# A Mamba-2 scan followed by a GELU feed-forward layer: batch transposes in two PSUM tiles, the last second-product by column halves, and a new instruction order

## The chip, the cores and the metric

The kernel runs on one core of one Trainium2 chip. The metric is device microseconds of that core, from an execution of the whole program, inputs and outputs in HBM. Lower is better. TensorE multiplies, VectorE (DVE), ScalarE (ACT) and GpSimd (POOL) do the elementwise work, and SyncE (SP) issues the DMA transfers.

## The reference

The program computes two layers, one after the other. First, a state-space scan over x (4 batches, 8 heads, 768 positions, 32 features), with decay a and matrices B and C (16 states each). A sequence is cut into chunks, and for each chunk

```
M       = (C B^T) * L                      # L[i,j] = product of a from j+1 to i, for i >= j, otherwise 0
y       = M x  +  (C state) * decay to i   # inside the chunk, and from the chunks before
state   = decay of the chunk * state + sum_j decay(j to end) * B_j x_j
```

Then y is laid out as 3072 tokens of 256 features, and

```
h   = y @ w_in                 # 256 -> 2048
g   = gelu_tanh(h)
out = g @ w_out                # 2048 -> 256
```

All inputs and the output are fp32; the kernel multiplies in bf16 and adds up in fp32.

## The kernel before

*Tiles.* A chunk is 128 positions, so a batch has 6 chunks and there are 24. Chunks go in units: the first two alone, then by twos, 13 units in all (`UNITS`, L126). A batch's decay is a running product (`f_clip`, `f_R`, `f_RT`, `f_recip`, L277 to L291), which VectorE multiplies into C and B of the whole batch (`f_mul`, L316, C first).

*One batch's preparation* (`sequence`, L607; `sequence0`, L628, for the first). TensorE transposes the scaled C and B (`f_T`: T_b_1 for C and T_b_0 for B, six 128x128 transposes each). For the batches after the first, both transposes go to banks 0 and 2 of one PSUM tile `gb` of four banks, by way of the list `T6` (L232). Evictions copy them to SBUF: `f_E` of C gives `ch`, of B gives `bh`. `f_F` makes `ce` from `ch`: two masked copies, one for even and one for odd heads. `f_N` transposes `bh` back chunk by chunk into bank 1 of `gb`, and `f_bn` evicts that as `bn`. For the first batch, `f_F0` reads the transposed C from PSUM directly, in two column ranges, and the transposes of B go to the one-bank tile `yb`.

*One unit.* `f_G` multiplies bh with ce into `gb`: the Gram matrices of the 8 heads, half of each bank for each chunk. `f_M` on VectorE multiplies them with the causal mask. `f_D` multiplies bn with x: the chunk's addition to the state. `f_S` and `f_SP` on VectorE carry the state on and spread it. `f_Y` adds the product of the states and of the masks into `yb`, and `f_yev` evicts that as `xm`, the input of the second layer. From unit 4 on, Y of a unit and D and G of the next are one node (YDG). `f_castx` turns a unit's x to bf16.

*The second layer.* `f_s1` multiplies a 128-row block of w_in's columns with a unit's tokens: groups of 512 output columns in one PSUM bank (pool `hp`, two banks; a few in the one bank of pool `o_ps`). `f_gelu` evicts each group on ScalarE. `f_s2` multiplies a chunk's g with w_out: 16 matmuls of 256 columns in four groups, into `o_ps` (two of the last four chunks: into `yb`). `f_oev` evicts them and `f_store` sends the chunk's 128 KB to HBM. The weights arrive as fp32 in two halves of w_in (1 MB each) and four quarters of w_out (512 KB each), and are cast in 512-column pieces (`f_wi`, `f_wo`: two pieces for each quarter of a matrix).

*The order.* Nothing is ordered by hand. Each step above is a node with an engine, a duration, dependencies and the buffers that it takes (`takes`, by pools with counts). `run_order` (L32) is a planner: it goes through planned time and, on each engine, takes of the nodes that can start the one with the lowest priority. The table `TUNE` gives each node its priority, `ENG` picks the engine for casts and evictions that may run on several. The outcome is the order in which instructions are emitted; each engine then runs its own in that order, and waits where a dependency asks for it. SP issues the loads in the planned order, and the stores in between. `emit_after` moves the emission of a batch's C eviction past the transpose of B. Where the plan has TensorE idle before the first product, filler matmuls with zero weights are put in (`idle`, L764).

Of the kernel before, what the change touches and what calls it, by code (L numbers as in the profile page):

```python
# [8 lines left out]
FP32 = mybir.dt.float32  # L9
BF16 = mybir.dt.bfloat16  # L10
# [4 lines left out]
class Node:  # L15


    def __init__(self, eng, dur, fn, deps=(), prio=0.0, done=0.0):
        self.eng, self.dur, self.fn, self.prio, self.done = eng, dur, fn, prio, done
        self.deps = [d for d in deps if d is not None]  # L20
        self.allocs = []
        self.after = 0.0
        self.emit_after = None
        self.start = self.end = None
# [7 lines left out]
def run_order(nodes, pools, hop=0.08, same=0.04, idle=None, wait=()):  # L32

    hist = {p: [] for p in pools}
    free = {}
    todo = list(nodes)
    order = []

    def est(n):
        t = 0.0  # L40
        for d in n.deps:
            if d.end is None:
                return None
            t = max(t, d.end + n.after
                    + (d.done + hop if d.eng != n.eng else 0.0 if n.eng == "PE" else same))
        for i, (pool, _) in enumerate(n.allocs):
            h, j = hist[pool], sum(p == pool for p, _ in n.allocs[:i])
            if len(h) + j >= pools[pool]:
                for d in h[len(h) + j - pools[pool]]:
                    if d.end is None:  # L50
                        return None
                    t = max(t, d.end + (same if d.eng == n.eng else hop))
        return t

    while todo:
        best = None
        cand = {}
        for n in todo:
            e = est(n)
            if e is not None:  # L60
                cand.setdefault(n.eng, []).append((e, n))
        assert cand, [(n.eng, n.prio, n.fn) for n in todo[:5]]
        for eng, c in cand.items():
            t = max(free.get(eng, 0.0), min(e for e, _ in c))
            if best is None or t < best[0]:
                best = (t, eng)
        t, eng = best
        ready = [(n.prio, e, i, n) for i, (e, n) in enumerate(cand[eng]) if e <= t + 1e-9]
        ready.sort(key=lambda r: r[:3])
        n = ready[0][3]  # L70
        if eng in wait:
            soon = [(e, m) for e, m in cand[eng] if t < e < t + n.dur - 0.1 and m.prio < n.prio - 5]
            if soon:
                e1 = min(e for e, _ in soon)
                fit = [r[3] for r in ready if t + r[3].dur <= e1 + 0.1]
                if fit:
                    n = fit[0]
                else:
                    t, n = min(((e, m) for e, m in soon if e <= e1 + 0.1),
                               key=lambda r: r[1].prio)  # L80
        if idle is not None and eng == "PE":
            x = idle(free.get(eng, 0.0), t)
            if x is not None:
                order.append((free.get(eng, 0.0), x, None))
        n.start, n.end = t, t + n.dur
        free[eng] = n.end
        for pool, by in n.allocs:
            hist[pool].append(by)
        todo.remove(n)
        order.append((t, n.fn, n))  # L90
    for n in nodes:
        if n.emit_after is not None:
            at = {r[2]: i for i, r in enumerate(order) if r[2] is not None}
            i, j = at[n], at[n.emit_after]
            if i < j and not any(r[2] is not None and r[2].eng == n.eng for r in order[i + 1:j]):
                order.insert(j, order.pop(i))
    return [(t, fn) for t, fn, _ in order]
# [3 lines left out]
def kernel(  # L101
# [10 lines left out]
    nc = tc.nc  # L112

    batch, H, S, D = x.shape
    N = B.shape[-1]
    Q = 128
# [115 lines left out]
    T6 = [gb[:, 2 * i, 0:S // 2].bitcast(BF16) for i in range(2)]  # L232
# [130 lines left out]
    def f_N(b, c0=0, c1=CPB):  # L363
        if c0 == 0:
            U[b]["n"] = (gb[:, 1] if b else psh.tile([128, 512], FP32, name="hp"))[:, 0:S // 2] \
                .bitcast(BF16)
        for c in range(c0, c1):
            nc.tensor.transpose(out=U[b]["n"][:, c * 128:(c + 1) * 128],  # L368
                                in_=U[b]["bh"][:, c * Q:(c + 1) * Q], identity=ident)
# [152 lines left out]

    def f_oev(gc, eng):
        o_sb = opool.tile([128, d_model], FP32, name="o_sb")
        if eng == "ACT":
            nc.scalar.activation(o_sb, ops.pop(gc), AF.Copy)  # L526
        else:
            nc.vector.tensor_copy(out=o_sb, in_=ops.pop(gc))  # L528
        outs[gc] = o_sb
# [40 lines left out]
    for item in FIRST.split() + [f"{t}{b}" if t in "CB" else f"x{CPB * b + int(t)}"  # L570
                                 for b in range(1, batch) for t in "CB012345"]:
        t, i = item[0], int(item[1:])
        if t in "CB":
            bl[i, int(t == "C")] = load(1.75, load_bc, i, int(t == "C"))
        elif t == "x":
            xl[i] = load(0.92, load_x, i)
        elif t == "i":
            win_l[i] = load(3.0, load_wi, i)
            win_l[i].done = 1.3
        else:  # L580
            won_l[i] = load(1.45, load_wo, i)
    cast = {"POOL": 0.6, "ACT": 0.62, "DVE": 0.45}
    for q in range(4):
        wi_n[q] = [add(cast, 0, f_wi, q, k, deps=[win_l[q // 2]], prio=-9 + 0.1 * q) for k in range(2)]
        wo_n[q] = [add(cast, 0, f_wo, q, k, deps=[won_l[q]], prio=20 + q) for k in range(2)]
    for h in range(2):
        win_l[h].takes("wf", *wi_n[2 * h], *wi_n[2 * h + 1])
        won_l[2 * h].takes("wf", *wo_n[2 * h], *wo_n[2 * h + 1])


    cl = add("DVE", 0.35, f_clip, deps=[an], prio=-90)
    R_ = add("DVE", 0.7, f_R, deps=[cl], prio=-89)
    RT_ = add("DVE", 0.53, f_RT, deps=[R_], prio=-88)
    rc1 = add("DVE", 0.47, f_recip, 0, 1, deps=[RT_], prio=-62)
# [12 lines left out]
    def sequence(b, after):  # L607
# [5 lines left out]
        tn[0].deps.append(tn[1])  # L613
        ev = {"DVE": 0.95, "ACT": 0.82}
        e1 = add(ev, 0, f_E, b, 1, 0, 128, deps=[tn[1], after], prio=q + 0.3)
        e1.emit_after = tn[0]
        e0 = add(ev, 0, f_E, b, 0, 0, 128, deps=[tn[0], after], prio=q + 0.5)
        ff = add("DVE", 0.74, f_F, b, deps=[e1], prio=q + 0.4)
        nn = add("PE", 0.34, f_N, b, deps=[e0, e1], prio=q + 0.6)
        bb = add({"ACT": 0.82, "DVE": 0.55}, 0, f_bn, b, 0, CPB, deps=[nn], prio=-45)  # L620
        tn[1].takes("gram", e1, e0)
        tn[1].takes("gram", e1, e0)
        nn.takes("gram", bb)
        nn.takes("gram", bb)
# [195 lines left out]
```

## Time and profile before

| | |
|---|---|
| median of 8 runs | 122.48 us (122.35 to 123.48) |
| the profiled execution's own time | 123.48 us |
| its span, from first to last instruction | 121.2 us |
| around the span | 2.28 us |
| TensorE busy | 111.3 us, 92% |
| ScalarE / VectorE / GpSimd busy | 75.6 / 63.5 / 20.1 us |
| DMA, the loads and stores together | 13.96 MB |
| last load landed | 53.32 us |
| last store landed | 120.15 us |

How to read the profile: times are microseconds from the span's start. "L502" is line 502 of the kernel. A group's name is the tile written, an arrow, and the tiles read. A row of the stretches gives its bounds, its length, then the busy time and number of instructions of PE (matmuls), PEld (weight loads), DVE, ACT and POOL, then TensorE's granted clock (1.00 is full), the mean busy share of the 16 DMA engines, and GB/s. A wait "A <- B" is idle time of A's engine that B ended. The chain is followed backwards from the last instruction, at each step to what released it. A matmul's row includes the time in which it drains, about 0.2 us; steps from one to the next are shorter than the duration.

### The profile page before, as it was taken

The page shows a single profiled execution, that of the slowest core. Times are in us where ns is not written, and L with a number is a line of the kernel's source. Part 1 is how long each engine was busy: PE and PEld are TensorE (multiplying, and loading weights), DVE is VectorE, ACT ScalarE, POOL GpSimd, SP SyncE. Part 2 cuts the span into 40 slices and gives each one's busy share as a digit, 9 for nine tenths or more (in the row PEclk, how much of TensorE's full clock was granted, in tenths as well). Part 3 has the DMA queues.
Part 4 walks back from the last instruction along what each step waited for, and adds up shares of the span by engine and source line. Part 5 has one row for each costly group of instructions (what it writes and reads, how often), then busy time and mean ns, then how long its engine had stood idle before and what let it go on. Part 6 is the DMA issues. An engine that isn't in the chain of part 4 may idle for free.

```text
span 121.2 us, 3506 instructions
## 1 busy us (share of the span) xinstructions
PE 111.3 (92%) x1507; PEld 98.2 (81%) x1507; DVE 63.5 (52%) x120; ACT 75.6 (62%) x143; POOL 20.1 (17%) x41
## 2 busy tenths in 40 slices
PE   4994959879899999999999999999999999999990
PEld 4993748758779898998889888897978999999970
DVE  5899677618579858907776719384745000000100
ACT  4138367554657686776866877766677778766410
POOL 7505078530240540222000000000000000000000
PEclk9999999999999999999999999999999999999999
DMA  1998999989999899851101101101110111011121
GB/s 46 277 319 174 300 270 300 267 186 227 217 214 165 137 213 239 136 108 50 43 2 49 43 1 49 43 0 49 43 49 0 43 43 40 12 43 43 43 87 43
DMA packets 38063, 13.96 MB, mean 115 GB/s; under 512 B 33824, under 2 KB 37024, under 8 KB 38048
## 3 DMA queue, kind: packets, MB, share of 16 engines
q1 hardware_dynamic: 37952, 13.69, 46.6%
q8 instruction: 11, 0.18, 0.6%
q10 hardware_dynamic: 96, 0.06, 0.2%
q14 instruction: 4, 0.03, 0.1%
HBM read 10.60 MB, written 3.15 MB: 113 GB/s over the span
## 4 chain that ended last, share of the span: by engine, by line
PE 75%; DMA 14%; SPq 3%; DVE 3%; ACT 2%; issue 1%; POOL 1%; DVEq 0%; POOLq 0%
PE hp L502 30%; PE o_ps L519 29%; DMA x_t<-in_x_dram 7%; DMA wf<-in_moe_w_in_dram 6%; PE yb L519 3%; PE gb L401 3%; PE yb L444 2%; PE yb L453 2%; PE gb L333 2%; DVE ch L266 2%; PE o_ps L783 1%; PE gb L368 1%; SPq L258 1%; SPq L159 1%; PE hp L422 1%
## 5 line engine op out<-in xcount | busy, mean ns | idle before, releaser
L510 ACT ACTIVATE gT<-hp 128x512 bf16<-128x512 f32 x94 | 52.7, 596 | 20.1 <-PE hp L502 19.8
L502 PE MATMUL hp<-xm,w_in_sb 128*128 128x256 bf16 (+1 forms) x400 | 51.3, 267 | 1.3 <-POOL w_in_sb L264 1.2
L519 PE MATMUL o_ps<-w_out_sb,gT 128*128 128x256 bf16 x352 | 47.6, 273 | 0.7 <-POOL w_out_sb L264 0.7
L502 PEld LDWEIGHTS <-w_in_sb 128*128 128x128 bf16 x416 | 41.9, 114 | 4.2 <-issue 1.6
L519 PEld LDWEIGHTS <-gT 128*128 128x128 bf16 x384 | 37.0, 98 | 5.4 <-issue 1.6
L411 DVE TENSOR_TENSOR m<-gb,tri 128x1024 bf16<-128x1024 f32 (+1 forms) x25 | 29.3, 1175 | 0.2
L528 DVE COPY o_sb<-o_ps 128x256 f32<-128x256 f32 x3 | 1.3, 425 | 26.3 <-PE o_ps L519 26.3
L264 POOL CAST x<-x_t 128x512 bf16<-128x512 f32 (+1 forms) x13 | 8.8, 682 | 23.8 <-DMA x_t<-in_x_dram 15.2
L471 DVE SCALAR_TENSOR_TENSOR s_new<-s_new,pend,hp 128x64 f32<-128x64 f32 x16 | 4.5, 279 | 12.6 <-PE hp L422 12.4
L783 PEld LDWEIGHTS <-wz 128*128 128x128 bf16 x105 | 7.7, 113 | 3.5 <-issue 1.8
L526 ACT ACTIVATE o_sb<-o_ps 128x256 f32<-128x256 f32 x19 | 7.3, 384 | 5.1 <-PE o_ps L519 2.8
L478 DVE SCALAR_TENSOR_TENSOR sp_new<-s_new,pend,bmask 128x256 bf16<-128x256 f32 x20 | 9.8, 490 | 0.1
L262 ACT ACTIVATE xm<-yb 128x512 bf16<-128x512 f32 (+1 forms) x13 | 7.3, 564 | 3.0 <-PE hp L422 2.6
L453 PE MATMUL yb<-m,x 128*32 128x128 bf16 x192 | 6.2, 220 | 0.0
L444 PE MATMUL yb<-ce,sp_new 128*32 128x128 bf16 x160 | 5.3, 221 | 0.0
L266 DVE COPY ch<-gb 128x768 bf16<-128x768 bf16 x3 | 2.9, 958 | 4.5 <-PE gb L333 4.5
L783 PE MATMUL yb<-wz 128*128 128x128 bf16 x35 | 3.7, 286 | 1.6 <-DVE warm L169 1.6
L264 POOL CAST w_out_sb<-wf 128x512 bf16<-128x512 f32 x7 | 4.5, 679 | 1.8 <-DMA wf<-in_moe_w_out_dram 1.8
L401 PE MATMUL gb<-ce,bh 32*128 32x256 bf16 x96 | 4.8, 273 | 0.0
L264 POOL CAST w_in_sb<-wf 128x512 bf16<-128x512 f32 x5 | 3.1, 664 | 9.2 <-DMA wf<-in_moe_w_in_dram 9.2
L469 DVE COPY s_new<-hp 128x64 f32<-128x64 f32 x4 | 0.9, 226 | 6.9 <-PE hp L422 6.9
L453 PEld LDWEIGHTS <-x 128*32 128x32 bf16 x192 | 3.7, 96 | 0.7 <-issue 0.6
(70 smaller groups left out, 64.7 us busy)
## 6 DMA issues: line engine op xcount, KB each, us to landing
x_t<-in_x_dram SPq DMA_DIRECT2D x24, 128.0 KB, 4.3
out_dram<-o_sb SPq DMA_DIRECT2D x24, 128.0 KB, 1.7
wf<-in_moe_w_in_dram SPq DMA_DIRECT2D x2, 1024.0 KB, 8.8
wf<-in_moe_w_out_dram SPq DMA_DIRECT2D x4, 512.0 KB, 6.6
bc_t<-in_C_dram SPq DMA_DIRECT2D x4, 384.0 KB, 4.5
bc_t<-in_B_dram SPq DMA_DIRECT2D x4, 384.0 KB, 5.2
a_t<-in_a_dram SPq DMA_DIRECT2D x1, 32.0 KB, 1.8
a_t<-in_a_dram ACTq DMA_DIRECT2D x1, 32.0 KB, 2.0
```

The lines of the kernel that those rows point to most:

```text
L262: nc.scalar.activation(o, i, AF.Copy)
L264: nc.gpsimd.tensor_copy(out=o, in_=i)
L401: nc.tensor.matmul(out=gb[:, g, 256 * k:256 * k + 256], lhsT=bh_of(gc)[32 * g:32 * g + 32], rhs=ce_of(gc)[32 * g:32 * g + 32], start=True, ...
L411: nc.vector.tensor_tensor(out=MT[gc][:, g0:g1], in0=gb[:, g0:g1, 256 * (k + half(u)):256 * (k + half(u)) + 256] .rearrange("p g (e t) -> p ...
L444: nc.tensor.matmul(out=y4[32 * j:32 * j + 32, k, w], lhsT=sp[:, 32 * h:32 * h + 32], rhs=ce_of(gc)[:, h % 2], start=first(j), stop=False, ...
L453: nc.tensor.matmul(out=y4[32 * j:32 * j + 32, k, w], lhsT=X16[u][:, k, 32 * h:32 * h + 32], rhs=m[:, h // 2, h % 2, :], start=first(j), st ...
L478: nc.vector.scalar_tensor_tensor(out=sp_new.rearrange("p (g d) -> p g d", g=4), in0=state[("s", gc)].rearrange("p (o d) -> p o d", o=1).to ...
L502: nc.tensor.matmul(out=hp[:, j * nt:(j + 1) * nt], lhsT=w_in_sb[:, kc].rearrange("p (q m k) -> p q k m", m=128, k=4)[:, fi // 4, fi % 4], ...
L510: nc.scalar.activation(gts[u][:, i * per:(i + 1) * per, 0:nt], hps.pop((u, i)).rearrange("p (j t) -> p j t", j=per), AF.Gelu_apprx_tanh)
L519: nc.tensor.matmul(out=ops[gc], lhsT=gts[u][:, fi, tt * Q:(tt + 1) * Q], rhs=w_out_sb[:, fi, :], start=(fi == 0), stop=(fi == NF - 1), ski ...
L526: nc.scalar.activation(o_sb, ops.pop(gc), AF.Copy)
L783: nc.tensor.matmul(out=bank[:, 384:384 + w], lhsT=wz[:, 0:128], rhs=r, start=True, stop=True)
```

## The change

- *PSUM tiles of the batch transposes.* For the batches after the first, the transposed B goes to `yb` and no longer to `gb`; N goes to `yb` as well. Only the transposed C stays in `gb`, and only the evictions of `ch` (one engine for each batch) and the masks read `gb`. The nodes take the matching pools. `emit_after` is gone.
- *The last chunk's second product* is made by halves of its columns: 16 matmuls of 128 columns into `o_ps`, then 16 into an `hp` bank, each half with its own eviction and its own 64 KB store.
- *Planned durations of the loads*: w_in's halves 2.6 and 3.4 instead of 3.0, their completion 1.25 instead of 1.3, that of w_out's quarters 1.2.
- *New priorities and engines* (`TUNE` and `ENG` are replaced as a whole), so that all engines' orders change up to about the sixth unit; from YDG_6 to the last chunk TensorE's order is the one of before.

The orders as they come out, where they matter most (SP's first loads; casts of weights, with the engine):

```
loads before:  C0 B0 w_in/0 x1 x0 w_in/1 x3 x2 w_out/0..3 x4 x5 C1 B1 x6 x7 B2 x8 x9 C2 ...
loads after:   C0 B0 x0 w_in/0 x1 w_in/1 x2 x3 x5 x4 w_out/0..3 C1 B1 x9 x6 x7 x16 x14 x8 x13 x10 x11 x12 x15 C2 B2 ...
POOL before:   wi_0_0 wi_1_0 x(0,1) wi_3_1 wi_2_1 wi_2_0 x(2) wo (7 pieces) x(3) ...
POOL after:    x(0) wi_0_0 wi_0_1 x(1) wi_1_1 wi_3_0 wi_2_1 x(2) x(3) wo (6 pieces) x(4) ...
w casts on ACT before: wi_0_1, wi_1_1 (ahead of and behind an eviction of ce)      after: wi_2_0 (behind gelu_0_1)
w casts on DVE before: wi_3_0, wo_3_1                                              after: wi_1_0, wi_3_1, wo_2_0, wo_3_0
TensorE before: ... D_2 G_3 s1_0_3 s1_1_2 Y_2 s2_0_0_0 s1_1_3 ... s1_2_4 s2_1_0_0 D_3 ... s1_2_7 Y_3 T_1_1 T_1_0 ... N_1 ... D_4 G_4
TensorE after:  ... s1_0_3 D_2 s1_1_2 G_3 Y_2 D_3 s1_1_3 s1_2_0 s1_2_1 s2_0_0_0 ... Y_3 s1_2_5 ... T_1_1 ... T_1_0 ... G_4 N_1 ... D_4
```

(s1_u_i is group i of the first product of unit u; s2_u_t_q quarter q of the second product of the unit's chunk t; wi_q_k and wo_q_k a piece of a weight's quarter q.) On VectorE, `mul_2_1` now stands behind the masks of unit 5 and ahead of S_6; the eviction of batch 1's C moved from VectorE to ScalarE.

The diff, without the two tables:

```diff
-    T6 = [gb[:, 2 * i, 0:S // 2].bitcast(BF16) for i in range(2)]
+    T6 = [yb[:, 0:S // 2].bitcast(BF16), gb[:, 2, 0:S // 2].bitcast(BF16)]
...
-            U[b]["n"] = (gb[:, 1] if b else psh.tile([128, 512], FP32, name="hp"))[:, 0:S // 2] \
+            U[b]["n"] = (yb if b else psh.tile([128, 512], FP32, name="hp"))[:, 0:S // 2] \
...
+    def f_s2_half(h, q):
+
+        u, w = NU - 1, d_model // 2
+        if q == 0:
+            ops["half", h] = (pso.tile([128, 512], FP32, name="o_ps") if h == 0 else
+                              psh.tile([128, 512], FP32, name="hp"))[:, 0:w]
+        for fi in range(4 * q, 4 * q + 4):
+            nc.tensor.matmul(out=ops["half", h], lhsT=gts[u][:, fi, Q:2 * Q],
+                             rhs=w_out_sb[:, fi, w * h:w * h + w], start=(fi == 0),
+                             stop=(fi == NF - 1), skip_group_check=True)
+
+    def f_oev_half(h, eng):
+        if h == 0:
+            outs["half"] = opool.tile([128, d_model], FP32, name="o_sb")
+        w = d_model // 2
+        copy(eng, outs["half"][:, w * h:w * h + w], ops.pop(("half", h)))
+
+    def f_store_half(h):
+        w = d_model // 2
+        nc.sync.dma_start(out=out[n_tokens - Q:, w * h:w * h + w],
+                          in_=outs["half"][:, w * h:w * h + w])
...
-            win_l[i] = load(3.0, load_wi, i)
-            win_l[i].done = 1.3
+            win_l[i] = load(2.6 + 0.8 * i, load_wi, i)
+            win_l[i].done = 1.25
         else:
             won_l[i] = load(1.45, load_wo, i)
+            won_l[i].done = 1.2
...
         e1 = add(ev, 0, f_E, b, 1, 0, 128, deps=[tn[1], after], prio=q + 0.3)
-        e1.emit_after = tn[0]
         e0 = add(ev, 0, f_E, b, 0, 0, 128, deps=[tn[0], after], prio=q + 0.5)
         ff = add("DVE", 0.74, f_F, b, deps=[e1], prio=q + 0.4)
-        nn = add("PE", 0.34, f_N, b, deps=[e0, e1], prio=q + 0.6)
+        nn = add("PE", 0.34, f_N, b, deps=[e0], prio=q + 0.6)
         bb = add({"ACT": 0.82, "DVE": 0.55}, 0, f_bn, b, 0, CPB, deps=[nn], prio=-45)
-        tn[1].takes("gram", e1, e0)
-        tn[1].takes("gram", e1, e0)
-        nn.takes("gram", bb)
-        nn.takes("gram", bb)
+        tn[1].takes("gram", e1)
+        tn[1].takes("gram", e1)
+        tn[0].takes("yb", e0)
+        nn.takes("yb", bb)
...
+            if gc == NCH - 1:
+                for h in range(2):
+                    for q in range(4):
+                        nd = add("PE", 0.226, f_s2_half, h, q, deps=[geln[u, 4 * n - 1], prev],
+                                 prio=PB + 45 + 10 * cs[0] + tt)
+                        if q == 0:
+                            first_n = nd
+                        prev = nd
+                    on = add({"DVE": 0.26, "ACT": 0.3}, 0, f_oev_half, h, deps=[prev], prio=-40)
+                    first_n.takes(("o", "hp")[h], on)
+                    sn = add("SP", 0.1, f_store_half, h, deps=[on], prio=gc)
+                    if h == 0:
+                        on.takes("ob", sn)
+                continue
```

## The prediction

> **What bounds the kernel now.** I read the page's shares first, then the busy times by stretch, then the chain that ended last, then who waited for whom, and last the tail.
>
> ```profile
> span 121.2 us, 3506 instructions
> PE 111.3 (92%) x1507; PEld 98.2 (81%) x1507; DVE 63.5 (52%) x120; ACT 75.6 (62%) x143; POOL 20.1 (17%) x41
> ```
>
> TensorE is busy 92% of the span; every other compute engine has a third or more to spare. The stretches (length, then busy time of PE, PEld, DVE, ACT, POOL, then clock, DMA share, GB/s) say where the missing 8% is:
>
> ```profile
> 15.90:17.90 2.00, 0.80 (x12) 0.54 (x10) 1.47 (x3) 1.37 (x3) 2.00 (x4) 1.00 0.96 296
> 17.90:26.55 8.65, 7.96 (x120) 6.60 (x120) 4.73 (x8) 5.17 (x10) 5.04 (x8) 1.00 0.92 258
> 26.55:35.85 9.30, 8.07 (x121) 6.70 (x120) 5.96 (x11) 5.39 (x10) 2.30 (x3) 1.00 1.01 219
> 35.85:54.59 18.74, 18.74 (x247) 16.84 (x246) 13.32 (x20) 13.30 (x25) 4.48 (x7) 1.00 0.93 166
> 54.59:117.92 63.33, 63.14 (x819) 56.58 (x818) 25.06 (x39) 43.35 (x83) 0.62 (x1) 1.00 0.11 37
> ```
>
> From 35.85 us to 117.92 us TensorE idles 0.2 us in all, at full clock: only less matmul work could shorten that. Between 15.90 and 35.85 it idles 1.20 + 0.69 + 1.23 = 3.1 us, while the DMA share is near 1. So the bound is loading first and TensorE afterwards, and an order can win what TensorE waits for before 36 us, plus the tail. Who ends those waits (total, times, longest):
>
> ```profile
> PE o_ps L783 <- ACT ce L350: 1.6, 1, 1.6
> PE hp L502 <- POOL w_in_sb L264: 1.2, 1, 1.2
> PE o_ps L519 <- POOL w_out_sb L264: 0.7, 3, 0.3
> PE hp L422 <- POOL x L264: 0.7, 1, 0.7
> PE gb L368 <- ACT bh L262: 0.6, 1, 0.6
> ```
>
> The chain (start, length, what) gives each its place:
>
> ```profile
> 10.43 0.63 ACT w_in_sb L262
> 11.06 0.58 ACT ce L350
> 11.69 1.11 PE o_ps L783 x17
> ...
> 17.71 8.86 DMA x_t<-in_x_dram
> ...
> 26.69 0.63 POOL x L264
> ...
> 31.67 0.97 DVE ch L266
> 32.66 0.82 ACT bh L262
> ```
>
> ScalarE took a weight cast that waited for w_in's first half (landed 10.41) ahead of the `ce` eviction; 17 filler matmuls waited behind that eviction. x of chunks 4 and 5 stood behind all of w_out and landed at 26.57, so D_3 waited. Batch 1's two evictions ran one after the other (`ch`, then `bh`), so N_1 waited.
>
> **The change, part by part.** I follow the new order on each engine, giving each instruction its row's duration, and compare the starts of the same TensorE blocks. Rows used: a 512-column group of first or second product 0.437; a two-chunk Y 0.45 to 0.56; T or N of six transposes 0.34; GELU 0.60; gram mask 1.22; S 0.28; SP 0.48; POOL cast 0.62; DVE cast 0.42; ACT cast 0.63; consumer about 0.2 after the last issue of its matmuls.
>
> *Landings.* Packets of one x load sum to 0.88 us of 16 engines, a B or C to 1.56, a w_out quarter to 1.58, a w_in half to 3.15. x0 now stands ahead of w_in's first half: 10.41 becomes at most 11.3, I take 11.2; x0 lands near 7.7. What precedes the second half is unchanged: 15.81. x4 and x5 move ahead of w_out and land near 18.7 instead of 26.6; the four quarters come 2 x 0.88 = 1.76 later, 20.5, 21.7, 24.1, 25.6. C1 and B1 follow the same bytes as before: 27.9 and 29.3.
>
> *Start.* The `ce` eviction no longer stands behind a weight cast, and no bn copy stands between the two halves of M_0 on VectorE: Y_0 moves from 13.03 to about 10.9. That is not the gain, for POOL now casts both parts of the first w_in quarter: 11.25 + 2 x 0.62 = 12.5, first product 12.55 instead of 13.89. Its third quarter waits for the landing at 15.81 as before. POOL has two casts of that half instead of three: 15.85 + 1.22 = 17.07, against 17.85. The ACT cast of it adds a wait: behind it on ScalarE stand the GELUs of chunk 1, ready near 15.2, now run 16.45 to 17.65; s1_0_2 needs the buffer freed at 17.05, no later than its weights, so this costs nothing, but it would if the landing slipped. s1_0_2 starts at 17.12. Then s1_0_3, D_2 (18.15), s1_1_2 (waits for a GELU, 18.3), G_3, Y_2 at 19.25 (before: 19.99, with the same work done): **-0.74**.
>
> *Middle.* D_3 comes at once, 19.8. s1_1_3 19.9, s1_2_0 20.65 (its xm eviction), s1_2_1 21.25, first second-product 21.8 (its w_out casts 20.5 + 1.24). Then no gap: Y_3 24.05 (masks end 23.5), s1_2_6 ends 25.45, s2_0_0_2 25.9. s2_0_0_3 needs casts of the last quarter, 25.65 + 0.62: 26.35, a wait of 0.45; ends 26.8. s1_2_7, s1_3_0, s2_1_0_0 end at 28.15. T_1_1 needs `mul_1_1` (0.90 from C1's 27.9): 28.85, a wait of 0.7. From there without a gap: s1_3_1, two groups, T_1_0 (30.55), three groups, G_4 32.25, N_1 ends 32.95; its `bh` eviction starts at 31.1 right after T_1_0, as `ch` now reads another PSUM tile and is done. By 35.85 the kernel before had the same done, and two groups and a D more (2 x 0.437 + 0.17 = 1.04). The new order is at that state at 32.95 + 1.04 = 33.99: **-1.86**, which holds the -0.74. The rest is the D_3 and N_1 waits, paid for with 0.45 and 0.7.
>
> *Until YDG_6* (54.59 before) both orders hold the same work, gapless before. Slack in the new one: the yb bank now serves T, N and Y in turn. YDG_5 at 43.0, T_2_0 at 48.8 (its mul ready 48.1), `bh` out at 50.45, N_2 50.9, its eviction by 52.4, YDG_6 52.75: the tightest slack is 0.4. *After YDG_6* the orders agree to the tail, except that batch 3's `ch` eviction need no longer wait for T_3_0; it removes the 0.17 wait at N_3: **-0.17**. Total matmul work is otherwise equal, filler excepted, which stands before the first product.
>
> *Tail.*
>
> ```profile
> 116.00 1.91 PE L519 MATMUL o_ps<-w_out_sb,gT 128*128 128x256 bf16 x16
> 118.00 0.42 DVE L528 COPY o_sb<-o_ps 128x256 f32<-128x256 f32 x1 [3.07 <-PE o_ps L519]
> ```
>
> 16 matmuls of 256 columns step at 109 ns: 1.75. Their place is taken by 32 of 128 columns, each with its own weight load. The nearest row is the transposes (fresh 128x128 weights, 128 columns): 12 in 0.67, 56 ns; first products of one chunk take up to 0.57 for 8, 71 ns. 32 x 60 = 1.92, +0.17 (+0.04 to +0.5). The Trainium skill, TensorE: Matmul & The Clock Gate, section Back-to-back issue gap, speaks against this part: a sustained stream of weight load and matmul pairs at N=128 is given as about 81 ns each, so 2.59 and +0.84. I take the trace. The first half's copy and store lie under the second's matmuls. The last copy shrinks: 128x256 took 425 ns, 128x64 226 (S from PSUM); a line through both gives 292: -0.13. The store took 1.37 from the end of its issue to landing; halving its bytes can spare only the data part. The skill's DMA: Bandwidth & Descriptors, in its table of the two cost components, gives a fixed part near 2.0 us, by which half the bytes spare 0.15; a whole store here took 1.7 with its issue, so that part is smaller here. I take -0.1 (0 to -0.3). Sum **-0.06** (+0.8 to -0.4).
>
> Sum: -1.86 - 0.17 - 0.06 = -2.09, some -2.0 as landings are known to a tenth at best. The profiled execution took 123.48 with a span of 121.2 (2.28 outside); the median is 1.00 below it. I put the change on the median: 122.48 - 2.0 = **120.5 us**.
>
> **Rivals.** *More:* C1 and w_out land early and the two waits (1.15) vanish: 119.4. For it: engine time of the bytes allows C1 1 us earlier; against it: landings have trailed it.
> *Half the gain:* x4 and x5 cost the w_out loads what they cost when they landed (23.82 to 26.57 = 2.75, not 1.76): every quarter another 1.0 later, TensorE waits for w_out at s2_0_0_3: 121.5. The scattered w_out row above speaks for it; against it, x2 and x3 added only 1.1.
> *No change:* waits move and do not vanish, since the same bytes must land and two hidden buffers alternate: GELUs held behind the ScalarE cast, and T_1 behind C1, return the 2.0: about 122.4. For it: until 29.3 us DMA runs near full in both. Against: by then TensorE waits for no later bytes.
> *Slower:* one mechanism. C2 and B2 are moved behind eleven x loads; `mul_2_1` stands ahead of S_6 and the next masks on in-order VectorE. C2 should land at 29.3 + 11 x 0.88 + 0.8 (two stores) + 1.56 = 41.4; VectorE reaches the mul at 41.8 and can wait to 42.8, with 0.4 more slack at N_2. From 43.2 each us late costs one; past 45.8 the kernel is slower by over 0.5%. At 46.2: 123.5. Against it: 4.4 us of lateness, more than any landing here strays.
>
> **How the numbers follow.** Forecast 0.55, more 0.06, half 0.12, no change 0.14, slower 0.13 (with all that makes VectorE or yb late in the like way). About 0.5% (0.61 us) is what a measurement of this kernel can tell from no change. Faster 0.55 + 0.06 + 0.12 = 0.73, same 0.14, slower 0.13. The forecast's own range, from its unknown costs (tail +0.8, slack, landings 0.5), is 119.7 to 121.5. The 8-in-10 range takes in more and half, and the near side of no change: 119.4 to 122.4.
>
> **What would show it.** Right: x waits on POOL near 26 us gone, no wait of D_3; second product's start near 21.8; N_1 and N_3 without a wait; TensorE idle between 15.9 and 33 us still about 2 us, on w_in, w_out and `mul_1_1`; YDG_6 near 52.8; the last 32 matmuls in about 1.9. Wrong: a wait of VectorE for C2 past 42.8; a wait of Y for yb; w_out waits over 1 us; 128-column matmuls stepping near 81 ns; w_in's second half landing after 16.5.

## The result and the profile after

The changed kernel took 121.27 us (median of 11, 120.38 to 122.21), beside 122.68 us for the kernel before in the same session (32 runs): ratio 0.9896, 95% interval 0.9865 to 0.9927, so 1.0% faster. The forecast was 120.5. Two more groups of runs gave 121.13 beside 122.41 (0.9897, 0.9825 to 0.9969) and 120.66 beside 122.57 (0.9834, 0.9784 to 0.9884). The ratios leave out executions that took over 1.5% more than the fastest of their kernel (1 of 12, 1 of 6 and 1 of 6 of the changed kernel); the medians hold them. The profiled execution took 121.33 us with a span of 119.5.

The page of the changed kernel: span, busy times, and the granted clock in 40 slices of 3 us.

```profile
span 119.5 us, 3521 instructions
...
PE 111.7 (93%) x1512; PEld 98.9 (83%) x1512; DVE 64.8 (54%) x121; ACT 76.6 (64%) x144; POOL 19.2 (16%) x40
...
PEclk9999959999999999999999999999999999999999
```

One slice has digit 5. The clock's record puts it at half speed for 3.41 us, from 14.47 to 17.89. No profile of the kernel before has such a window between start and last matmul.

Stretches of the changed kernel, columns as in the prediction (bounds, length, busy PE, PEld, DVE, ACT, POOL, clock, DMA share, GB/s):

```profile
10.00:14.00 4.00, 2.26 (x33) 1.46 (x30) 3.25 (x6) 1.35 (x4) 2.09 (x4) 1.00 1.06 337
14.00:18.00 4.00, 3.92 (x55) 2.96 (x56) 2.37 (x5) 1.71 (x3) 2.17 (x4) 0.57 0.90 152
18.00:22.00 4.00, 3.69 (x93) 3.07 (x90) 3.64 (x8) 3.22 (x6) 1.68 (x3) 1.00 0.99 334
22.00:36.00 14.00, 13.76 (x171) 12.14 (x170) 9.94 (x16) 11.04 (x20) 4.22 (x7) 1.00 0.97 210
36.00:55.00 19.00, 19.00 (x289) 16.79 (x288) 13.48 (x23) 13.60 (x26) 4.41 (x7) 1.00 0.87 185
55.00:114.00 59.00, 59.00 (x748) 53.48 (x745) 24.17 (x37) 41.42 (x79) 0.32 (x1) 1.00 0.10 33
```

After 36 us TensorE has no gap at all, where the kernel before still lost 0.2, and from 22 to 36 it loses 0.24. Between 14 and 18 us it is busy for 3.92 of 4.00 at a clock of 0.57: a group of the first product inside the window starts 0.81 before the next (17.01 to 17.82), where the same group took 0.44 at full clock in a second profile of this kernel.

TensorE's waits (total, times, longest):

```profile
PE o_ps L812 <- DVE w_in_sb L259: 0.9, 1, 0.9
PE o_ps L812 <- POOL w_in_sb L257: 0.8, 1, 0.8
PE yb L326 <- DVE bc L314: 0.3, 1, 0.3
PE hp L495 <- DVE s_new L464: 0.2, 1, 0.2
```

The waits for `x` (0.7), for w_out's casts (0.7) and for `bh` (0.6) are gone. Two waits stand ahead of filler matmuls (L812), which the new order places among the casts of w_in's first half; the last four stand behind the second POOL cast, ahead of the first product.

The chain of the changed kernel around the start (start, length, what):

```profile
3.48 8.37 DMA wf<-in_moe_w_in_dram
...
11.91 1.63 POOL w_in_sb L257 x2
13.54 0.04 issue
13.58 0.40 PE o_ps L812 x4
13.98 0.05 issue
14.02 0.69 PE o_ps L495 x8
...
15.90 0.61 ACT gT L503
...
18.06 0.61 ACT gT L503
...
18.70 0.61 PE hp L495 x8
```

The two POOL casts took 1.63, not 1.24, and the third quarter's product began at 18.70, behind a GELU that waited for products at half clock.

The tail of the changed kernel, in order of time (start, length, engine, line, tiles, shapes):

```profile
114.22 1.06 PE L523 MATMUL o_ps<-w_out_sb,gT 128*128 128x128 bf16 x16
...
115.11 1.06 PE L523 MATMUL hp<-w_out_sb,gT 128*128 128x128 bf16 x16
115.37 0.29 DVE L259 COPY o_sb<-o_ps 128x128 f32<-128x128 f32 x1 [2.22 <-PE o_ps L523]
...
116.20 0.29 DVE L259 COPY o_sb<-hp 128x128 f32<-128x128 f32 x1 [0.55 <-PE hp L523]
```

Sixteen matmuls of 128 columns start 0.89 apart from the next sixteen: 55.6 ns each.

### The profile page after: what moved, and what is told of

The parts are those of the page before. It is cut to its first block, busy times and chain, and to the rows that moved or that the text cites. A ratio compares the mean times of both kernels' runs of the same rounds, so it can differ in the third digit from the quotient of the medians.

```text
span 119.5 us, 3521 instructions
## 1 busy us (share of the span) xinstructions
PE 111.7 (93%) x1512; PEld 98.9 (83%) x1512; DVE 64.8 (54%) x121; ACT 76.6 (64%) x144; POOL 19.2 (16%) x40
## 4 chain that ended last, share of the span: by engine, by line
PE 82%; DMA 7%; DVE 2%; SPq 2%; POOL 1%; ACT 1%; issue 1%
PE hp L495 35%; PE o_ps L512 31%; DMA wf<-in_moe_w_in_dram 7%; PE yb L512 3%; PE gb L394 2%; PE yb L437 2%; PE yb L446 2%; POOL w_in_sb L257 1%; DVE sp_new L471 1%; ACT gT L503 1%; PE o_ps L495 1%; PE yb L361 1%; PE gb L326 1%; PE yb L326 1%; SPq L152 1%; PE hp L415 1%
## 5 line engine op out<-in xcount | busy, mean ns | idle before, releaser
L503 ACT ACTIVATE gT<-hp 128x512 bf16<-128x512 f32 x94 | 52.6, 595 | 16.2 <-PE hp L495 15.9
L495 PE MATMUL hp<-xm,w_in_sb 128*128 128x256 bf16 (+1 forms) x400 | 52.4, 270 | 0.6 <-DVE s_new L464 0.2
L512 PE MATMUL o_ps<-w_out_sb,gT 128*128 128x256 bf16 x336 | 45.2, 273 | 0.0
L512 PEld LDWEIGHTS <-gT 128*128 128x128 bf16 x368 | 35.8, 98 | 3.8 <-issue 0.2
L543 DVE COPY o_sb<-o_ps 128x256 f32<-128x256 f32 x2 | 0.8, 425 | 23.5 <-PE o_ps L512 23.5
L257 POOL CAST x<-x_t 128x512 bf16<-128x512 f32 (+1 forms) x13 | 8.1, 625 | 26.8 <-DMA x_t<-in_x_dram 19.5
L812 PEld LDWEIGHTS <-wz 128*128 128x128 bf16 x94 | 7.0, 112 | 3.8 <-issue 1.9
L255 ACT ACTIVATE xm<-yb 128x512 bf16<-128x512 f32 (+1 forms) x11 | 6.4, 578 | 3.0 <-PE hp L415 2.1
L812 PE MATMUL yb<-wz 128*128 128x128 bf16 x47 | 4.4, 268 | 1.6 <-DVE warm L162 1.6
L437 PEld LDWEIGHTS <-sp_new 128*32 128x32 bf16 x160 | 2.9, 96 | 1.8 <-issue 1.6
L314 DVE TENSOR_TENSOR bc<-bc_t,rt 128x768 bf16<-128x768 f32 x4 | 3.8, 955 | 0.7 <-DMA bc_t<-in_B_dram 0.7
```

What stands on the lines that cost most here:

```text
L255: nc.scalar.activation(o, i, AF.Copy)
L257: nc.gpsimd.tensor_copy(out=o, in_=i)
L437: nc.tensor.matmul(out=y4[32 * j:32 * j + 32, k, w], lhsT=sp[:, 32 * h:32 * h + 32], rhs=ce_of(gc)[:, h % 2], start=first(j), stop=False, ...
L495: nc.tensor.matmul(out=hp[:, j * nt:(j + 1) * nt], lhsT=w_in_sb[:, kc].rearrange("p (q m k) -> p q k m", m=128, k=4)[:, fi // 4, fi % 4], ...
L503: nc.scalar.activation(gts[u][:, i * per:(i + 1) * per, 0:nt], hps.pop((u, i)).rearrange("p (j t) -> p j t", j=per), AF.Gelu_apprx_tanh)
L512: nc.tensor.matmul(out=ops[gc], lhsT=gts[u][:, fi, tt * Q:(tt + 1) * Q], rhs=w_out_sb[:, fi, :], start=(fi == 0), stop=(fi == NF - 1), ski ...
```

## The experiments

For each profile I split the time up to TensorE's last matmul into two sums: *work*, the union of all its matmuls except fillers, and *idle*, the rest (fillers count as idle). A half clock under products lengthens the work, a wait lengthens the idle.

| profile | w_in 2nd half landed | first product | Y_2 | last product | idle | work | half clock before the tail | span |
|---|---|---|---|---|---|---|---|---|
| before, the first | 15.81 | 13.89 | 19.99 | 116.00 | 14.00 | 103.91 | 0 | 121.2 |
| before, again | 15.38 | 13.71 | 19.64 | 114.51 | 12.58 | 103.84 | 0 | 119.7 |
| changed, the first | 16.16 | 14.02 | 20.87 | 114.22 | 11.65 | 104.52 | 3.41 | 119.5 |
| changed, again | 15.50 | 13.64 | 19.38 | 113.03 | 11.38 | 103.60 | 0 | 118.7 |
| cast on ScalarE | 15.54 | 12.64 | 19.15 | 112.74 | 11.04 | 103.65 | 0 | 118.2 |
| casts split | 15.82 | 13.16 | 19.57 | 113.10 | 11.46 | 103.60 | 0 | 118.5 |
| more fillers | 16.48 | 14.17 | 19.91 | 114.17 | 12.57 | 103.54 | 0 | 119.5 |
| all reorderings | 16.96 | 13.67 | 20.30 | 115.47 | 13.44 | 103.98 | 0 | 120.9 |
| loads alone | 15.97 | – | – | 118.01 | 15.54 | 104.38 | 0 | 123.2 |
| x4, x5 late | 15.25 | – | – | 120.39 | 15.18 | 107.16 | 10.24 | 126.1 |
| old placement, new plan | 16.99 | – | – | 117.57 | 13.70 | 105.81 | 3.41 | 123.1 |
| old placement alone | 16.43 | – | – | 116.42 | 13.05 | 105.32 | 3.41 | 121.7 |

### The two kernels again

> The changed kernel once more, as the yardstick for the runs beside it. Every theory: 1.0 to 1.5 us below the kernel before. If its lost clock (half speed for 3.4 us around 15 us) is a matter of chance, some executions show a granted clock of 1.00 and some 0.986 or 0.972.

> The kernel before, unchanged, for a second profile and a second set of times. Theory (the change saves two microseconds once the loads of w_in stand where they stand; the first profile of before was one of its slower executions outside the span and had early loads): the span less the landing of w_in's second half is again 105 to 105.5 us, so a span near 120.4 goes with a landing near 15.0 to 15.4. Rival (the change saves only what the medians show, 0.9 us in the span, and the 2.0 is chance of one profile): the landing is 15.8 or later and the difference is 104.6 or less.

> The changed kernel once more, as the reference of its neighbours in this group of runs: 121.1 to 121.6 us, 0.9 to 1.2% faster than before; idle of TensorE outside the fillers 11.3 to 11.7 us, all of it before 25 us.

The changed kernel gave 121.13 and 120.66, as told with the ratios above; the second is below the 121.1 to 121.6 that was expected. The kernel before, run against itself, gave 122.85 beside 122.55 (ratio 1.0018, 0.9987 to 1.0049). Its second profile has a span of 119.7, less landing of w_in's second half 104.3: the rival's number, not the theory's 105 to 105.5, though the rival's landing of 15.8 or later did not come either (15.38). What differs is seen in its waits:

```profile
PE o_ps L783 <- ACT ce L350: 1.4, 1, 1.4
PE hp L502 <- POOL w_in_sb L264: 0.8, 1, 0.8
PE gb L368 <- ACT bh L262: 0.6, 1, 0.6
PE o_ps L519 <- POOL w_out_sb L264: 0.2, 1, 0.2
PE gb L368 <- DVE bh L266: 0.2, 1, 0.2
```

The first profile's waits for `x` (0.7) and most of those for w_out (0.7) don't occur here; those of N_1 and N_3 (`bh`, 0.6 and 0.2) do. The first profile is one of the longer executions: 121.2, where the median span of 68 executions of the kernel before is 120.7. The second is among the shortest. The changed kernel's idle is 11.4 to 11.65, against 12.6 and 14.0. Between the two second profiles, both at full clock and with landings 0.12 apart (15.38 and 15.50), the change gains 1.2 in the idle and 1.0 in the span.

The two kernels' executions that the ratios count, sorted by mean granted clock:

| | executions | span | time |
|---|---|---|---|
| before, clock 0.99 or more | 47 | 120.7 | 122.54 |
| before, below 0.99 | 21 | 120.7 | 122.53 |
| changed, clock 0.99 or more | 13 | 118.8 | 120.65 |
| changed, below 0.99 | 8 | 119.65 | 121.37 |

Among executions with the clock kept, the changed kernel's are 1.9 us shorter; among those with a window, 1.1 to 1.2. (Half speed for 3.41 us takes 1.7 us from full speed, 1.4% of the span, so a mean of 0.986 is one window.) The kernel before does not get longer when its mean falls; where its windows lie no profile showed. In the changed kernel's first profile the window lies at 14.47 to 17.89, on the first products, and work is 104.52 where the second profile has 103.60. The third quarter's product came 2.54 behind its weights' landing there, and 1.72 in the second profile: 0.8 lost. That profile's landing was 0.66 later too, so the 0.85 between the last two rows need not be the window's alone; landings are known for profiled executions only. The third profile of the changed kernel fell into an execution with twice that window (6.83 us, from 12.88) and a landing at 16.29, and its span isn't used; its waits were the same two casts of w_in, and its idle 11.37.

### More fillers, to keep the clock

```diff
+    def more():
+        for _ in range(36):
+            nc.tensor.matmul(out=state["spare"][:, 384:512], lhsT=wz[:, 0:128], rhs=wz[:, 0:128],
+                             start=True, stop=True)
+    i = [r[2] for r in seq].index("Y_0") + 1
+    seq[i:i] = [(0.0, more, "more")]
```

> The changed kernel with 36 more filler matmuls right behind Y_0, where TensorE idles about 2 us for w_in's first casts. They write a bank that nobody reads. Theory (the idle time there is what halves the clock from 14.5 to 17.9 us, and loads have 0.25 to 0.6 us of slack behind that): granted clock 1.00 in all executions, the third quarter's product about 0.5 to 1 us earlier, the time 0.3 to 0.5 us below the changed kernel's. Rival (the clock falls by chance, or its fall is hidden behind w_in's second half): no difference in time.

121.70 us, ratio 0.9935 (0.9895 to 0.9975): not faster than the changed kernel (121.13 in that group). The clock stayed full in 11 of 12 executions, and the third quarter's product began at 17.75, 0.95 earlier than in the changed kernel's first profile, as expected; the time did not follow. Fillers took 10.75 us of TensorE instead of 8.1 to 8.4, and the idle (fillers counted in) was 12.6 instead of 11.4 to 11.65. But w_in's second half landed at 16.48, and the third quarter's product began only 1.27 behind it, so the fillers did not hold it. So the clock can be kept there; whether the fillers' price or the late landing ate what it saves, this run doesn't show.

### One of w_in's first casts on ScalarE

```diff
     def f_wi(q, k, eng):
+        if (q, k) == (0, 1):
+            eng = "ACT"                 # and its place: right behind yev_0
```

> The changed kernel with one of the two casts of w_in's first quarter on ScalarE, right behind the first xm eviction, instead of on GpSimd behind the other one. First product at about 12.7 us instead of 14.0, the third quarter's product at about 17.3 instead of 18.7. Theory (two limits in series: behind the start stand the w_out and C1 landings with 0.25 to 0.6 us of slack): 0.3 to 0.6 us faster than the changed kernel, and new TensorE waits on w_out or on the product for T_1 between 25 and 30 us. Rival (the start sets the end alone): 1.2 to 1.4 us faster. Second rival (w_in's second half sets it): no difference.

121.34 us, 0.9889 (0.9819 to 0.9959): no difference. The first product did start at 12.64, 1.0 earlier than in the changed kernel's second profile. Then:

```profile
PE hp L497 <- ACT gT L505: 0.8, 1, 0.8
```

ScalarE's own timeline in that stretch (the bracket is idle before, and what ended it):

```profile
15.56 0.63 ACT L255 ACTIVATE w_in_sb<-wf 128x512 bf16<-128x512 f32 x1 [0.97 <-DMA wf<-in_moe_w_in_dram]
16.10 1.07 ACT L505 ACTIVATE gT<-hp 128x512 bf16<-128x512 f32 x2
```

ScalarE stood 0.97 us before a cast whose weights landed at 15.54, with GELUs behind it in the queue; TensorE waited for their buffers. Most of the microsecond won at the first product is spent there: the third quarter began at 16.73, 0.49 earlier than in the changed kernel's second profile, and Y_2 at 19.15, only 0.23 earlier.

### Casts split, no GELU behind a cast that waits

```diff
     def f_wi(q, k, eng):
+        eng = {(0, 1): "ACT", (2, 0): "DVE", (3, 1): "ACT"}.get((q, k), eng)
...
+    put("wi_0_1", "yev_0", 1)
+    put("wi_2_0", "wi_3_1", 0)
+    put("wi_2_1", "wi_3_0", 0)
+    put("wi_3_1", "gelu_1_1", 1)
```

> The changed kernel with other engines for the casts of w_in: one of the first half on ScalarE, the first of the third quarter on VectorE, one of the fourth quarter on ScalarE behind the two GELUs of the second group of 256 instead of ahead of them. Theory (once no GELU stands behind a cast that waits for a landing, the third quarter's product is 0.8 to 1.0 us behind the landing of w_in's second half, not 1.2 to 1.7): 0.4 to 0.8 us faster than the changed kernel, no wait of TensorE for a GELU between 15 and 18 us. Rival (the landing and its first cast set it, the rest is taken up by the next wait): within 0.3 us.

120.86 us, 0.9871 (0.983 to 0.9912), beside 120.66 for the changed kernel in the same group: no difference, the rival's outcome. The wait for a GELU is gone; in its place:

```profile
PE hp L496 <- DVE w_in_sb L259: 0.8, 1, 0.8
```

and on VectorE's timeline:

```profile
15.40 1.21 DVE L405 TENSOR_TENSOR m<-gb,tri 128x1024 bf16<-128x1024 f32 x1
16.53 0.79 DVE L259 CAST w_in_sb<-wf 128x512 bf16<-128x512 f32 x1
```

The weights had landed at 15.82, but VectorE was in a mask until 16.53, and the cast took 0.79. The third quarter began at 17.38, 1.56 behind the landing, hardly better than 1.72 in the changed kernel. The queue that is late has moved from ScalarE to VectorE.

### All reorderings together

The first cast on ScalarE, wi_2_0 on VectorE, the third quarter's casts first, and in the first group:

```diff
+    put("s1_2_7", "s2_0_0_2_o", 0)
+    put("gelu_2_7", "s2_0_0_2_o", 0)
+    put("yev_3", "wo_3_0", 0)
+    put("T_1_1", "s1_3_1", 1)
+    put("gelu_3_1", "T_1_1", 0)
```

> The changed kernel with another order of the casts and of the first group's second products: one cast of w_in's first half on ScalarE, the casts of the third quarter ahead of those of the fourth on VectorE and on GpSimd, the last first-product and GELU of group 2 ahead of the second product that needs w_out's third quarter, the transpose of chunk 1 one step later. Theory (the casts' order and ScalarE's queue hold the third quarter's product some 0.5 us behind its landing, and the waits for w_out and for chunk 1 bind once that is gone): the first product of the third quarter starts 1.3 us after w_in's second half has landed instead of 1.9 to 2.1, no wait for w_out; 0.4 to 0.8 us faster than the changed kernel (120.4 to 120.8 where that is 121.2). Rival (landings alone set the start): within 0.2 us of the changed kernel.

122.32 us, 0.9951 (0.992 to 0.9982): 0.5% faster than before, 1 us or more slower than the changed kernel in the other groups, against both expectations. The third quarter did start 1.01 behind its landing. But w_in's halves landed at 12.45 and 16.96, x5 at 21.07 (19.22 and 19.61 in the changed kernel's profiles), and D_3 waited 0.9 for its cast. The idle is 2 us above the changed kernel's. Why the loads landed later is open; the order of their issue is the changed kernel's.

### The loads, alone and left out

x4 and x5 ahead of w_out in the kernel before, and nothing else:

```diff
+    early = [r for r in seq if r[2] in ("ad_x_4", "ad_x_5")]
+    seq = [r for r in seq if r not in early]
+    i = min(j for j, r in enumerate(seq) if r[2].startswith("ad_wo_"))
+    seq[i:i] = early
```

> The kernel before with one edit of the change alone: the loads of x4 and x5 are issued ahead of the four quarters of w_out; everything else as before. Theory (the load order gains nothing alone): the w_out quarters land some 1.8 us later than before, the second products of the first group wait for them, D_3's wait for x is gone; 0.5 to 1.2 us slower than before (122.9 to 123.7 where before is 122.4). Rival (the load order is what makes the change's gain): 0.8 to 1.3 us faster than before.

124.72 us, 1.0151 (1.0099 to 1.0203): 2.2 us slower, twice what was expected. The w_out quarters landed at 20.56, 22.42, 25.20 and 26.57, against 18.96 to 23.06 in the second profile of before, so 1.6 to 3.7 later, not 1.8, and TensorE waited for them:

```profile
PE o_ps L519 <- POOL w_out_sb L264: 2.8, 5, 1.2
```

The reverse, the changed kernel with x4 and x5 behind w_out (the four w_out loads, then x4 and x5, all put behind `gelu_1_1` in the order of emission; w_out's first quarter then landed at 17.79):

> The changed kernel with the loads of x4 and x5 issued behind the four quarters of w_out, as before the change; each engine's order kept. Theory (order of work and order of loads belong together): x for D_3 lands at about 24.5 instead of 19.6 us, D_3 stands in TensorE's queue at 20.0, so TensorE stands 3.5 to 5 us there; 2 to 4.5 us slower than the changed kernel, slower than before too. Rival (the earlier w_out repays it, and the order of work makes the gain whatever the loads): within 0.5 us of the changed kernel.

128.17 us, 1.0456 (1.0404 to 1.0509): 7.5 us slower than the changed kernel in that group, more than the 2 to 4.5 expected. x5 landed at 24.62 as expected, and D_3 waited as expected:

```profile
PE hp L415 <- POOL x L257: 4.5, 1, 4.5
```

Beside the changed kernel's second profile the idle is 3.8 longer, within the expectation. The surplus is in the work, 107.16 instead of 103.60, with the clock at half speed from 23.97, inside that wait, to 30.79 (6.83 us), and in an earlier window of 3.41 us from 13.73. Neither half of this pair gains alone: load order and work order are one edit.

### The old placement

With the old pools the planner also plans anew:

```diff
-    T6 = [yb[:, 0:S // 2].bitcast(BF16), gb[:, 2, 0:S // 2].bitcast(BF16)]
+    T6 = [gb[:, 2 * i, 0:S // 2].bitcast(BF16) for i in range(2)]
...
-            U[b]["n"] = (yb if b else psh.tile([128, 512], FP32, name="hp"))[:, 0:S // 2] \
+            U[b]["n"] = (gb[:, 1] if b else psh.tile([128, 512], FP32, name="hp"))[:, 0:S // 2] \
...
-        nn = add("PE", 0.34, f_N, b, deps=[e0], prio=q + 0.6)
+        nn = add("PE", 0.34, f_N, b, deps=[e0, e1], prio=q + 0.6)
```

> The changed kernel with the old placement in PSUM: the two heads' masked transposes in one tile of the Gram's bank and N in that bank as before; the new order of the work, the loads and the halved last product stay. Theory (the order of the work makes the gain, the placement only removes the short waits of N): 0.2 to 0.6 us slower than the changed kernel, still 0.6 us or more faster than before; one or two waits of TensorE for the reading of the Gram bank, 0.1 to 0.4 us each, come back. Rival (the placement makes the gain): within 0.3 us of before.

124.49 us, 1.0122 (1.0084 to 1.0159): 3.2 us above the changed kernel's first median, where 0.2 to 0.6 was expected (what the expectation calls the two heads' transposes are those of C and B). The profile shows a cause that is not the placement itself. VectorE's timeline:

```profile
43.11 0.96 DVE L321 TENSOR_TENSOR bc<-bc_t,pt 128x768 bf16<-128x768 f32 x1 [2.71 <-DMA bc_t<-in_C_dram]
43.99 0.27 DVE L471 SCALAR_TENSOR_TENSOR s_new<-s_new,pend,hp 128x64 f32<-128x64 f32 x1
```

and TensorE's:

```profile
45.03 1.06 PE L502 MATMUL hp<-xm,w_in_sb 128*128 128x256 bf16 x8 [1.09 <-DVE s_new L471]
```

The new plan let VectorE reach C2's multiplication 2.71 us before C2 landed (43.09); the state update behind it freed TensorE's buffer 1.09 late. That is the prediction's slower rival, at a landing that hurts little in the changed kernel's first profile: there C2 landed at 42.51, VectorE waited 0.20, and the state update after it waited for TensorE anyway.

So the placement was put back once more with every engine's order kept: only the two tile lines above. This kernel leaves out what keeps N apart from the Gram: N is written over a part that VectorE has not read, so it does not compute those chunks' outputs. Its instructions and their order are those of the changed kernel.

> The changed kernel with every engine's order of instructions kept as it is and the old placement alone put back: both heads' masked transposes in the Gram's tile, N there too. Theory (the placement saves the two waits of N that both traces of before show, 0.55 and 0.17 us): 0.5 to 0.9 us slower than the changed kernel, the waits back at N_1 and N_3. First rival (the 3 us that the version with a newly planned order lost were the placement's own): 2 us or more slower. Second rival (the new order covers the waits anyway): within 0.3 us.

123.57 us, 1.0065 (1.0018 to 1.0112), 2.9 us above the changed kernel of the same group. Waits of TensorE from 20 to 70 us:

```profile
PE gb L326 <- DVE ch L259: 0.8, 2, 0.6
PE hp L495 <- DVE s_new L464: 0.6, 1, 0.6
PE hp L415 <- ACT gT L503: 0.5, 1, 0.5
```

The transposes of B now wait for the eviction of C out of the same tile (0.61 at 50.8 us, 0.17 at 67.7). At 36.4 D_4 waits 0.53 for a GELU. ScalarE's and VectorE's timelines show why:

```profile
35.08 0.81 ACT L255 ACTIVATE bn<-gb 128x768 bf16<-128x768 bf16 x1 [1.62 <-DVE m L404]
35.92 1.23 DVE L404 TENSOR_TENSOR m<-gb,tri 128x1024 bf16<-128x1024 f32 x1 [0.88 <-ACT bn L255]
```

The eviction of N out of the Gram's tile stood 1.62 behind unit 4's first mask, with GELUs behind it on ScalarE, and the second mask stood behind that eviction. The 0.61 for `s_new` lies at 22.6, ahead of the first transposes that the placement touches; the changed kernel lost 0.2 there.

How much the placement costs is read by laying this profile beside the changed kernel's first one: it has the same order of matmuls and a half-clock window of the same 3.41 us. T_1 starts 0.30 later (29.49 beside 29.19), before the placement can act. D_4 starts 0.90 later (36.43 beside 35.53), T_2_0 1.87 later (50.82 beside 48.95), T_3_0 2.21 later (67.73 beside 65.52), and the spans end 2.2 apart. So the old placement costs 1.9 us in this order, more than the 1.3 counted as waits, since a matmul's row holds its draining too. The two executions with a full clock say much the same: 122.40 and 123.07, beside a median of 120.53 for the changed kernel's five at full clock in that group. The theory (0.5 to 0.9) missed; the first rival (2 us or more, the placement's own) comes nearest. In the kernel before the same placement costs 0.72 in waits (N_1 and N_3), in an order that was planned for it.

### The last chunk whole

The branch `if gc == NCH - 1:` is taken out of the changed kernel, so 16 matmuls of 256 columns, one copy and one store are left.

> The changed kernel with the last chunk's second product whole, as before. Theory (the last matmuls cost nothing as halves, the copy and the store get shorter): the last store lands about 0.3 us later, counted from the start of the last chunk's product, and the time is 0.3 us longer than the changed kernel's. Rival (128-column matmuls step near 81 ns): it is 0.3 to 0.8 us shorter.

121.55 us, 0.9911 (0.987 to 0.9951); the changed kernel had 121.13 in that group. From the start of the last product, matmuls end after 1.91 us whole and 1.95 by halves; the last store lands after 4.15 whole, and after 3.83 to 4.25 by halves (3.9 or less in six of the ten such profiles). So the halves win 0.3 at best, as expected, and lose 0.1 at worst. The medians can't show it: 9 of 12 executions of the whole version had a mean clock below 0.99, against 11 of 24 of the changed kernel.

## Why the prediction was right, and where not

**The total.** 121.27 us lies above the forecast of 120.5, and inside its range. Among executions at full clock the sum of -2.0 is met: 122.54 - 120.65 = 1.9 us. That it is met so closely is partly luck, as the paragraph on the median shows. What failed is the unspoken step that the clock stays full. A third to a half of the changed kernel's executions have a mean clock below 0.99; no term of the sum has it, and no rival spoke of it. Over all executions the gain is 1.3 to 1.9 by session. The window is not the whole of the 0.8 between the first median and the forecast: in that group the five executions at full clock have a median of 120.89, the six with a window that the ratio counts 121.30. The rest is open; later landings of w_in, at 16.16 and 16.29 in the profiles with a window where 15.81 was predicted, are one candidate.

**Landings.** In the first and second profile w_in's first half came at 11.86 and 11.47 (predicted 11.2), the second at 16.16 and 15.50 (15.81), x5 at 19.61 and 19.22 (18.7), the last w_out quarter at 26.27 and 25.51 (25.6), C1 at 27.65 and 26.95 (27.9).

**Start, -0.74.** At full clock Y_2 came at 19.38, -0.61; with the window at 20.87, +0.88. Inside it one term was wrong and did not matter. "11.25 + 2 x 0.62" for POOL was 11.91 + 1.63, because the landing was later and a POOL cast took 0.80 to 0.87 beside VectorE's casts and state steps. The profile of before had such rows: of its 12 POOL casts of weights three took 0.81 to 0.87. Four fillers behind the second cast, which the prediction left out, took 0.4 more. The first product came at 13.64 to 14.02, no earlier than before, instead of 12.55. But the third quarter's product, which waits for the other landing, began at 17.22 where 17.12 was predicted, and in the ScalarE cast experiment a first product 1.0 earlier brought Y_2 forward by 0.23 only. The remark that the ScalarE cast "costs nothing, but would if the landing slipped" describes the 0.8 us wait of that experiment.

**Middle, -1.86 with the start, then -0.17.** The waits of D_3, N_1 and N_3 went, as predicted. The two waits charged for them, 0.45 for w_out's last quarter and 0.7 for C1, did not come. In the full-clock profile the last quarter's piece was cast by VectorE in 0.43 after landing at 25.51, done at 25.95 just as TensorE arrived, and C1 landed 0.95 earlier than estimated, `mul_1_1` ending at 27.93 with T_1_1 at 28.01. With the clock window TensorE was later than both. So its idle from 15.9 to 33 us was 0.43 and 0.60, not the 2 that was named as a sign, and YDG_6 came at 52.02, or 53.21 with the window (52.75 predicted). Against the first profile this made the idle fall by 2.62 where 2.03 was predicted (start and middle).

**Setting the sum on the median.** The first profile of before held 0.7 for x and 0.7 for w_out that the second lacks or has at 0.2, and its span is 0.5 above the median one. Shifting its whole gain to the median was generous by that, and the two absent waits made it good: two errors of opposite sign, each about half a microsecond, and so luck. Between the two second profiles, with like landings, the gain is 1.0 in the span.

**Tail, -0.06.** The matmuls: +0.04 (+0.17 predicted; 55.6 ns measured, 60 assumed). The 81 ns that the Trainium skill gives (TensorE: Matmul & The Clock Gate, Back-to-back issue gap) is not seen here; by an estimate from it the block would have taken 2.59. The copy: 0.29, as predicted. The last store took 1.52 to 1.58 from the start of its issue to landing in the ten profiles with halves, and 1.70 whole, so 0.12 to 0.18 are spared where 0.1 was taken. The 0.15 that the prediction had worked out from the Trainium skill's table fits; that table's fixed part near 2.0 us (DMA: Bandwidth & Descriptors, Anatomy of one DMA) is given for transfers that GpSimd issues, and these are SP's. The last landing, counted from the start of the product: 0.32 earlier to 0.10 later. But the program's end after that landing took 1.00 in all three profiles made from the kernel before, and 1.40 to 1.55 in all those made from the changed one, the whole tail's too. So the span kept nothing of it. The traces place most of the surplus in one gap among GpSimd's closing instructions: its second semaphore instruction starts 0.41 to 0.44 behind its first in eight of the eleven, 0.08 to 0.09 in the kernel before (in the three with a first cast on ScalarE the gap comes later). What it waits for there is open.

**Rivals.** "More" had the right reason (TensorE did not wait for w_out and C1), but its 119.4 was not reached: the lowest time was 119.58. "Half the gain" by dearer loads: w_out's landings cost 1.6 to 3.7 when the loads were moved alone, but in the changed kernel's first two profiles they came within 0.9 of the prediction and no wait followed. "No change" did not come. "Slower" through C2 is real, as the newly planned old placement showed, but not in this order of work.

## What to carry to other kernels

Before putting a gain worked out of one profile on a median, look at a second profile of the same kernel: here half of the waits to be removed were in one and not in the other. Look at the granted clock behind a start of waits with few fillers between them: here six of the seven profiles of such kernels have their first products at half clock. Order of loads, order of work and buffer placement were one edit: the loads or the placement, put in or taken out alone, cost 1.9 to 7.5 us, though all of them together gain 1.3 to 1.9, so a part's worth can't be read from its share of the diff.

## What the runs showed of the hardware

- The half-clock window of 3.41 us began at 13.7 to 15.6 us in five of the profiles with the changed kernel's fillers, behind TensorE's gaps at 11.4 to 14 us. Of the kernels that keep those fillers and casts (the changed one, the whole tail and the two old placements), 35 of 55 executions had a mean clock below 0.99; of those that fill or shift that stretch (more fillers, and the three with a first cast on ScalarE), 4 of 36. That is a correlation over kernels, and a mean does not tell where the window lies; what sets it was not tried apart.
- A POOL cast of 128x512 took 0.61 us beside a mask on VectorE, and 0.80 to 0.87 beside VectorE's casts and state steps; a VectorE cast of that size took from 0.41 to 0.88. Of two such casts that begin almost together, the second takes longer: 0.43 on VectorE from 11.88 and 0.87 on POOL from 11.91 (changed, the first), 0.62 on POOL from 17.02 and 0.88 on VectorE from 17.04 (all reorderings).
- The same issue order landed w_in's second half from 15.25 to 16.99 over the profiles of the changed kernel and its near versions. Nothing in the traces told why.
- Outside the span lay 1.7 to 1.9 us in every execution of the changed kernel (24), but over 1.98 in 22 of 74 of the kernel before (up to 2.87; its first profile 2.28). It isn't explained, and with medians of 1.71 and 1.75 it doesn't explain the gain.
